# A hand-written list of steps in another order: gated linear attention on one core

## The chip, the core and the metric

The kernel runs on one core of one Trainium2 chip. The core has five engines with an instruction queue each, and each queue is worked off in its own order: TensorE (PE) for matmuls, VectorE (DVE), ScalarE (ACT) and GpSimd (POOL) for work on elements, and SyncE (SP), which here only issues DMAs. An instruction starts when its engine has come to it and the semaphores that it waits for are set. The metric is the time of one execution in microseconds (us), the median of several runs.

## The reference

```python
q_s = softmax(q, over head_dim);  k_s = softmax(k, over seq)      # with 1e-9 in the sums
kv  = einsum('bhsd,bhse->bhde', k_s, v)
x   = einsum('bhsd,bhde->bhse', q_s, kv)        # then heads side by side: (B, S, 512)
gate_pre[s] = sum over k = 0..4 of conv_w[k] * x[s + k - 4]       # causal, per channel
gate = 1 / (1 + exp(-gate_pre))
out  = (gate * (x @ w_val)) @ w_out
```

There are 8 batches, 8 heads, 576 positions and a head size of 64, all in float32.

## The kernel before

**Work and tiling.** Channels lie on partitions: the 512 channels are four blocks of 128, so x, gate, value and output of one batch are four tiles of 128 x 576 each. A batch goes through these stages: load q, k, v; maxima, exponentials and sums (`q_max`, `q_sub`, `q_exp`, `q_sum`, `k_peak`, `k_sub`, `k_exp` and others); `kv` on PE; `attend` on PE, which leaves two blocks of x in PSUM; then for each block a cast of x to the type that the large products take (`x_high`), the rest that the cast lost (`x_low`, on DVE), and the convolution. The latter is one scaled copy (`first`) and four multiply-adds (`tap`, on DVE), of which some are split into a scaled copy on ACT (`far`) and an addition on POOL (`near`). `sigmoid` follows on ACT. `value` multiplies x with `w_val` on PE, `gated` multiplies the result with the gate on DVE, `g_high` and `g_low` split this product as x was split, `project` multiplies it with `w_out` on PE, `copy` brings the result to SBUF and `put` stores it. Each of the large products takes 24 matmuls: high times low, high times high and low times high parts of four blocks, in two halves of the positions.

**The first batch differs.** Its channel blocks 0 and 1 get their convolution on PE (`conv`, 80 matmul records), and the two weight matrices are decoded from 64-bit words while it runs: eight slabs of 128 columns, 0 to 3 of `w_val` and 4 to 7 of `w_out`, each through `field`, `scaled`, `signed` (two DVE instructions), `part`, `joined`, and then `w_high` and `w_low`. Slab m is needed by `value 0 m`, or `project 0 m-4`. Twelve matmuls on ones (`warm`) stand at PE's start.

**What sets the order.** A list `ORDER` of some 1000 steps is written out in the code, and the program issues step after step as it stands there; nothing is scheduled behind it. A step is a name, a batch or slab, a block or part, and for many steps a letter for its engine: `x_high 4 1 a` casts block 1 of batch 4 on ACT, `v` stands for DVE and `p` for POOL. As every engine works off its own queue in order, the list sets for each engine what stands behind what. A second table, `HOMES`, says for each new tile which of its buffers it takes; a step that writes a buffer waits for the last reader of the tile that lay there. PSUM is four such buffers ("banks"), shared by all of PE's results, so that a product can be held up by whoever still reads the bank that it is to get: `conv`, for instance, takes the banks of x blocks 0 and 1 of batch 0 and waits for their `x_low`.

Lines that the profile names (before's numbers): `field` L282, `scaled` L204 on ACT and L206 on POOL, `signed` L291 and L292, `joined` L295, `k_raise` L380, `q_max` L415, `q_sub` L420, `q_exp` L424, `q_each` L499, `q_eps` L435, `q_mul` L506, `kv` L521, `q_turn` L546, `attend` L580, `first` L593 on ACT and L595 on DVE, `x_low` L600, `tap` L605, `value` and `project` L630, `conv_kv` L661, `conv` L676, `gated` L689, `g_low` L697. Casts and copies (`x_high`, `g_high`, `w_high`, `q_turned`, `k_turned`) are L198 on ACT and L200 elsewhere, the scalings of `copy` L204 on ACT.

Of the kernel before, what the change touches and what calls it, by code (L numbers as in the profile page):

```python
# [16 lines left out]
B, H, S, D = 8, 8, 576, 64  # L17
C = H * D
P = 128
# [22 lines left out]
    kv_sums 0, field 2 p, kv_norm 0 v, conv_kv, load_words 7, load_kc 1 2, part 2 a, q_turn 0 0, q_turned 0 0 a,
    scaled 2 p, signed 2, joined 2 p, q_turn 0 1, q_turned 0 1 a, w_high 1 a, q_max 1 0 2, attend 0 0, w_low 1 p,
    x_high 0 1 a, x_low 0 1, x_high 0 0 a, q_sub 1 1 p, x_low 0 0, q_max 1 2 4, attend 0 1, first 0 2 a, load_words 6,
    x_high 0 3 a, load_v 1, first 0 3 a, tap 0 3 3, w_high 3 p, tap 0 3 1, part 0 a, x_high 0 2 a, field 4 p,
    tap 0 3 0, q_each 1 3, conv, field 5 p, x_low 0 3, scaled 5 p, tap 0 3 2, joined 0 p, w_high 0 p, w_low 0 p,
    x_low 0 2, q_each 1 2, part 5 a, conv_gate 1, k_top 1 1, k_raise 1 1, conv_gate 0, k_top 1 3, k_raise 1 3,
    w_low 3 p, load_vt 4, k_top 1 0, k_raise 1 0, k_top 1 2, scaled 4 a, load_km 2 3, signed 5, joined 5 p,
    load_q 2 0 5, k_raise 1 2, value 0 1, q_sum 1 2 4, tap 0 2 3, w_high 2 a, value 0 0, gated 0 1, gated 0 0,
    q_sub 1 0 p, part 4 a, k_tail_turn 1, k_tail_turned 1 v, field 6 p, k_peak 2 3, q_exp 1 1 2, w_low 2 p,  # L50
    g_high 0 0 a, q_eps 1 2 4 a, q_rec 1 2 4, signed 4, k_turn 1 1, joined 4 p, k_turn 1 0, q_exp 1 0 1, q_sum 1 0 2,
    k_turned 1 0 a, load_km 3 0, q_eps 1 0 2 p, tap 0 2 0, k_peak 2 0, q_rec 1 0 2, load_k 2, g_high 0 1 a, field 7 p,
    scaled 6 a, g_low 0 0 p, k_peak 2 1, q_mul 1 0 p, w_high 5 a, value 0 2, w_high 4 a, w_low 4 p, k_turned 1 1 a,
    kv 1, q_mul 1 1 a, tap 0 2 1, tap 0 2 2, sigmoid 0 2, q_mul 1 2 p, kv_sums 1, value 0 3, g_low 0 1 p, q_mul 1 3 a,
    kv_norm 1 v, q_max 2 0 5, gated 0 2, load_km 3 2, scaled 7 a, load_km 5 3, load_v 2, q_turn 1 0, sigmoid 0 3,
    q_turn 1 1, tail_high 1 a, q_turned 1 0 a, gated 0 3, w_low 5 p, signed 6, g_high 0 2 a, g_low 0 2 v,
    g_high 0 3 a, attend 1 0, x_high 1 0 a, k_peak 3 2, first 1 0 v, g_low 0 3 p, tap 1 0 2, q_sub 2 3 p, load_kt 2,
    k_row 2, q_sub 2 4 p, tap 1 0 3, part 6 a, tap 1 0 1, q_turned 1 1 a, load_q 3 0 5, x_high 1 1 a, first 1 1 a,
    project 0 1, copy 0 1 a a, joined 6 p, q_sub 2 2 p, tap 1 0 0, project 0 0, w_high 6 a, x_low 1 0, w_low 6 p,
    load_km 5 0, tap 1 1 0, load_k 3, tap 1 1 2, put 0 1, part 7 a, x_low 1 1, signed 7, copy 0 0 a a, attend 1 1,  # L60
    project 0 2, sigmoid 1 0, far 1 2 2, x_high 1 2 a, x_high 1 3 a, joined 7 p, w_high 7 a, q_sub 2 1 p, tap 1 1 3,
    first 1 3 a, tap 1 1 1, sigmoid 1 1, w_low 7 p, k_spread 2, q_sub 2 0 p, k_sub 2 3 p, k_sub 2 1 p, k_peak 3 0,
    k_peak 5 0, k_sub 2 0 p, copy 0 2 a a, load_v 3, tap 1 3 3, x_low 1 3, x_low 1 2, value 1 0, q_exp 2 0 5, put 0 0,
    first 1 2 a, q_max 3 0 4, load_km 3 1, project 0 3, k_sub 2 4 p, gated 1 0, copy 0 3 a a, q_sum 2 0 5,
    q_eps 2 0 5 a, load_km 3 3, value 1 1, k_sub 2 2 p, put 0 2, load_km 4 3, k_peak 3 3, kt_exp 2, load_km 4 2,
    load_km 4 1, load_vt 2, k_peak 3 1, q_rec 2 0 5, k_row 3, k_exp 2, tap 1 2 0, load_km 4 0, tap 1 2 3, q_mul 2 4 a,
    q_mul 2 1 a, gated 1 1, tap 1 2 1, tap 1 3 2, tap 1 3 0, tap 1 3 1, sigmoid 1 3, g_high 1 0 p, load_km 5 1,
    q_sub 3 2 p, k_peak 4 3, value 1 3, kv 2, kv_sums 2, kv_norm 2 v, tail_turn 2, tail_turned 2 a, q_sub 3 0 p,
    k_peak 4 2, g_high 1 1 a, q_mul 2 2 p, q_mul 2 0 p, q_mul 2 3 p, q_turn 2 0, q_sub 3 1 p, g_low 1 0 p,
    q_turned 2 0 a, q_sub 3 3 p, k_peak 4 1, near 1 2 2, k_peak 5 3, put 0 3, gated 1 3, value 1 2, g_low 1 1 p,  # L70
    q_exp 3 0 4, q_turn 2 1, k_spread 3, k_peak 5 1, k_peak 4 0, sigmoid 1 2, gated 1 2, tail_high 2 a,
    q_turned 2 1 a, q_total 3, attend 2 0, far 2 1 0, first 2 0 v, tap 2 0 1, load_km 5 2, q_log 3, load_v 4,
    tap 2 0 3, load_qc 3 3, g_high 1 3 p, g_low 1 3 p, g_high 1 2 p, g_low 1 2 p, load_km 6 1, load_km 6 2, tap 2 0 2,
    l_turn 3, project 1 3, first 2 1 a, load_q 4 0 5, copy 1 3 a a, near 2 1 0, k_row 4, x_high 2 1 a, far 2 1 3,
    tap 2 1 2, put 1 3, x_low 2 1, x_high 2 0 a, x_low 2 0, load_qc 3 1, near 2 1 3, l_row 3, project 1 0,
    copy 1 0 a a, project 1 2, k_sub 3 3 p, tap 2 1 1, sigmoid 2 1, k_sub 3 4 p, far 2 0 0, k_sub 3 2 p, near 2 0 0,
    q_max 4 0 5, copy 1 2 a a, load_qc 3 0, q_sub 4 4 p, put 1 0, k_peak 6 1, attend 2 1, q_sub 4 3 p, first 2 2 a,
    tap 2 2 1, x_high 2 2 v, kt_exp 3, x_high 2 3 a, q_sub 4 1 p, first 2 3 a, tap 2 3 0, q_sub 4 2 p, x_low 2 2,
    project 1 1, copy 1 1 a a, q_sub 4 0 p, x_low 2 3, l_spread 3, sigmoid 2 0, q_exp 4 0 5, value 2 1, tap 2 2 0,
    tap 2 2 2, k_sub 3 0 p, k_sub 3 1 p, k_exp 3, load_kt 4, tail_high 3 a, l_sub 3 0 p, load_k 4, tap 2 3 1,  # L80
    gated 2 1, g_high 2 1 a, tap 2 3 3, k_peak 6 2, tap 2 3 2, k_spread 4, c_exp 3 0, value 2 0, load_qc 3 2,
    l_sub 3 3 p, g_low 2 1 p, sigmoid 2 3, gated 2 0, load_qc 4 1, value 2 3, q_total 4, c_exp 3 3, gated 2 3, kv 3,
    value 2 2, kv_sums 3, load_q 5 0 5, k_peak 5 2, tap 2 2 3, kv_norm 3 v, l_sub 3 1 p, q_log 4, c_exp 3 1,
    attend 3 0, load_km 6 3, g_high 2 0 a, sigmoid 2 2, g_high 2 3 p, g_low 2 3 p, first 3 1 a, l_turn 4, gated 2 2,
    first 3 0 v, load_vt 6, far 3 1 0, k_row 5, tap 3 0 3, g_low 2 0 p, tap 3 0 1, g_high 2 2 p, put 1 1, g_low 2 2 p,
    project 2 0, x_high 3 1 v, l_sub 3 2 p, load_km 6 0, project 2 1, load_qc 4 3, tap 3 1 2, x_low 3 1, k_sub 4 3 p,
    put 1 2, c_exp 3 2, k_sub 4 4 p, copy 2 0 a a, tap 3 1 1, tap 3 1 3, x_high 3 0 a, l_row 4, copy 2 1 a a,
    q_max 5 0 4, k_sub 4 1 p, put 2 0, far 3 0 0, attend 3 1, load_qc 5 1, first 3 3 a, k_sub 4 2 p, first 3 2 a,
    q_sub 5 1 p, k_peak 6 3, x_high 3 3 a, put 2 1, k_sub 4 0 p, project 2 2, tap 3 0 2, q_sub 5 2 p, load_qc 4 0,
    l_spread 4, x_high 3 2 a, x_low 3 0, k_exp 4, x_low 3 3, tap 3 2 3, k_peak 6 0, project 2 3, copy 2 2 a v,  # L90
# [713 lines left out]
```

## Time and profile before

| | before |
|---|---|
| median of 3 runs | 287.61 us (287.55 to 287.83) |
| the profiled execution's own time | 287.65 us |
| its span, first to last instruction | 285.9 us |
| busy PE / DVE / POOL / ACT | 278.8 / 231.7 / 205.8 / 192.8 us |
| instructions DVE / ACT / POOL | 329 / 322 / 191 |
| moved by DMA | 62.93 MB |

The span is what the trace holds; 1.75 us of the execution lie outside it. Times in the trace count from the start of the span. PE's busy time holds the time in which a matmul waits behind the one in front of it, so "busy" alone does not tell whether PE works at its pace; the distance between the starts of its groups does.

### The profile page before, as it was taken

How to read it: one execution, taken by the hardware profiler on the slowest of the kernel's cores; microseconds unless marked ns; L12 is line 12 of the kernel's file. 1: busy time of each engine (PE TensorE's matmuls, PEld its weight loads, DVE VectorE, ACT ScalarE, POOL GpSimd, SP SyncE). 2: the span in 40 equal slices, each digit the busy share in tenths (PEclk: the TensorE clock that was granted, in tenths of full speed). 3: DMA queues.
4: the chain of work that ended last, by engine and by line, in shares of the span. 5: the costliest groups of instructions: out<-in, count | busy, mean ns of one | idle time of the engine just before them, and what ended most of it. 6: DMA issues, size and time to landing. Idle time of an engine off the chain costs nothing.

```text
span 285.9 us, 6653 instructions
## 1 busy us (share of the span) xinstructions
PE 278.8 (98%) x2640; PEld 250.6 (88%) x2640; DVE 231.7 (81%) x329; ACT 192.8 (67%) x322; POOL 205.8 (72%) x191
## 2 busy tenths in 40 slices
PE   8988999999999999999999999999999999999995
...
GB/s 241 397 414 399 316 226 301 214 416 346 84 262 345 250 284 128 332 198 224 371 417 257 211 225 322 287 165 126 153 182 159 217 0 2 44 41 85 0 83 85
DMA packets 23463, 62.93 MB, mean 220 GB/s; under 512 B 3432, under 2 KB 3976, under 8 KB 20744
## 3 DMA queue, kind: packets, MB, share of 16 engines
...
q14 instruction: 10, 0.08, 0.1%
...
## 4 chain that ended last, share of the span: by engine, by line
PE 84%; DVE 7%; ACT 2%; issue 1%; POOL 1%; DVEq 0%
PE val L630 36%; PE out_a L630 32%; PE kv L521 6%; PE x L580 5%; PE cv L676 2%; DVE gate L605 2%; DVE x L600 1%; PE qTps L546 1%; DVE e L292 1%; DVE kpk L340 1%; PE kps L387 1%; ACT q L506 1%; PE out_r L630 1%; PE out_l L630 1%; POOL f L295 0%
## 5 line engine op out<-in xcount | busy, mean ns | idle before, releaser
L630 PE MATMUL val<-x,w_val_hi 128*128 128x288 f32 x512 | 89.1, 295 | 0.1
L605 DVE SCALAR_TENSOR_TENSOR gate<-x,cw,gate 128x575 f32<-128x575 f32 (+3 forms) x98 | 78.8, 809 | 5.7 <-ACT gate L593 2.2
L630 PEld LDWEIGHTS val<-x,w_val_hi 128*128 128x128 f32 x512 | 75.3, 188 | 0.3 <-DVE x L600 0.3
L630 PE MATMUL val<-x,w_val_lo 128*128 128x288 f32 x256 | 56.1, 300 | 0.0
L630 PE MATMUL out_a<-gh,w_out_lo 128*128 128x288 f32 x248 | 54.6, 301 | 0.0
L630 PE MATMUL out_a<-gh,w_out_hi 128*128 128x288 f32 x248 | 53.2, 296 | 0.0
L697 POOL TENSOR_TENSOR gl<-g,gh 128x576 fp32r<-128x576 f32 x24 | 34.6, 1443 | 14.7 <-ACT gh L198 8.0
L630 PEld LDWEIGHTS out_a<-gh,w_out_lo 128*128 128x128 f32 x248 | 39.4, 188 | 5.7 <-issue 1.8
L630 PE MATMUL out_a<-gl,w_out_hi 128*128 128x288 f32 x248 | 43.0, 295 | 0.0
L614 POOL TENSOR_TENSOR gate<-gate,far 128x572 f32<-128x572 f32 (+3 forms) x22 | 29.1, 1324 | 18.7 <-DVE gate L605 10.0
L630 PEld LDWEIGHTS val<-x,w_val_lo 128*128 128x128 f32 x256 | 40.7, 188 | 1.6 <-DVE g L689 0.4
L630 PEld LDWEIGHTS out_a<-gh,w_out_hi 128*128 128x128 f32 x248 | 39.8, 188 | 0.0
L204 ACT ACTIVATE o<-out_a 128x576 f32<-128x576 f32 x27 | 17.6, 650 | 31.6 <-PE out_a L630 22.0
L630 PEld LDWEIGHTS out_a<-gl,w_out_hi 128*128 128x128 f32 x248 | 36.4, 188 | 0.0
L420 POOL TENSOR_TENSOR q<-q,qm 128x512 f32<-128x512 f32 x32 | 33.5, 1062 | 3.6 <-DVE qm L415 3.5
L689 DVE SCALAR_TENSOR_TENSOR g<-gate,val 128x576 f32<-128x576 f32 x32 | 23.8, 749 | 13.8 <-PE val L630 5.9
L490 POOL TENSOR_TENSOR qc<-qc,lb 128x576 f32<-128x576 f32 (+1 forms) x17 | 24.1, 1428 | 11.0 <-DMA lb<-lrow 11.0
L355 POOL TENSOR_TENSOR k<-k,kmax 128x512 f32<-128x512 f32 x23 | 30.2, 1330 | 0.2
L617 ACT ACTIVATE gate<-gate 128x576 f32<-128x576 f32 x30 | 20.2, 683 | 8.3 <-DVE gate L605 8.0
L600 DVE TENSOR_TENSOR x<-x,x 128x576 fp32r<-128x576 f32 x32 | 23.1, 749 | 1.7 <-ACT x L198 1.6
L610 ACT ACTIVATE far<-x,cw 128x572 f32<-128x572 f32 (+3 forms) x22 | 16.2, 737 | 9.2 <-PE x L580 4.0
L424 ACT ACTIVATE q<-q 128x512 f32<-128x512 f32 (+2 forms) x11 | 15.9, 1442 | 8.8 <-POOL q L420 8.8
(108 smaller groups left out, 456.4 us busy)
## 6 DMA issues: line engine op xcount, KB each, us to landing
...
```

Of the source, the lines that this page charges most:

```text
L204: nc.scalar.mul(out, in_, factor)
L355: engine(e).tensor_sub(kk[r, cs], kk[r, cs], mx[r, cs])
L420: engine(e).tensor_tensor(qq, qq, m, op=ALU.add if b < 2 else ALU.subtract)
L490: engine(e).tensor_sub(t, t, T["lb", b][:, p])
L521: nc.tensor.matmul(acc[h * D:(h + 1) * D, p, :], T["k", b][:, c, cs] if c < 4 else ktz[b % 2][:, cs], T["v", b][:, c, hd] if c < 4 else T[ ...
L600: nc.vector.tensor_sub(xl, T["x", b, p], T["xh", b, p].bitcast(F32))
L605: nc.vector.scalar_tensor_tensor(out=a, in0=x, scalar=w, in1=a, op0=ALU.mult, op1=ALU.add)
L614: nc.gpsimd.tensor_add(a, a, T["far", b, p, j])
L617: nc.scalar.activation(T["gate", b, p], T["gate", b, p], AF.Tanh, scale=0.5)
L630: nc.tensor.matmul(ps[:, cs], a[:, kb, ms], z[:, cs], start=(i == 0), stop=(i == len(parts) - 1))
L689: nc.vector.scalar_tensor_tensor(out=T["g", b, m], in0=T["gate", b, m], scalar=1.0, in1=T["val", b, m], op0=ALU.add, op1=ALU.mult)
L697: engine(e).tensor_sub(T["gl", b, m], T["g", b, m], T["gh", b, m].bitcast(F32))
```

## The change

The list gets another order, and 78 of its steps another engine letter. No step is added or dropped, except that `warm` issues 11 matmuls instead of 12. Of the 78 steps, 37 come to DVE and 20 leave it, so DVE has 17 instructions more; the other 21 trade places between ACT and POOL. The list is arranged so that few `tap` steps, casts and sums stand directly behind the step whose result they read on the same engine. `HOMES` is written anew to fit the order. A second copy of the function `warm` (the same text) comes into the file; lines behind it have a number higher by five. The numbers of matmuls, DMAs and bytes stay as they are, except for that one warming matmul.

```diff
 ORDER = [step.strip() for step in """
-    warm 12, load_words 3, field 3 p, load_q 0 2 5, load_kc 0 0, load_q 0 0 1, load_taps, scaled 3 p, signed 3,
+    warm 11, load_words 3, load_q 0 2 5, load_kc 0 0, load_q 0 0 1, load_taps, load_q 0 1 2, load_ident, part 3 a,
...
-    q_mul 0 0 p, part 1 a, q_mul 0 1 a, k_peak 2 2, tail_turned 0 a, conv_rows, tail_high 0 a, joined 1 p, kv 0,
+    tail_turned 0 a, signed 0, k_peak 2 2, load_kc 1 0, kv 0, kv_sums 0, w_high 3 a, load_kc 1 1, q_mul 0 0 p,
...
 HOMES = {
     "bank": (
-        "012303102130231213213120130212310101023023102021303013021312303013012303012323021312310101231230"
-        "101203032012303013230123012"
+        "012303023012310310310302310231230303102123012120131031023132101013210323123030312020321212012103"
+        "232130301320101203023120312"
     ),
...
+    def warm(n):
+        ps = bank("warm")[:D, :512].rearrange("p (n d) -> p n d", d=D)
+        for _ in range(n):
+            nc.tensor.matmul(ps, ones, ones.unsqueeze(1).broadcast_to([P, 512 // D, D]), start=True, stop=True)
```

At three places the program's own order shows what moved. The first is DVE's start, before the change; e3 and f3 are weight slab 3 in decoding, qm the maxima of q, and q0 the first batch's q:

```order
L291 TENSOR_SCALAR e3_110<-e3_110 128x512
L292 SCALAR_TENSOR_TENSOR e3_110<-words3_108,e3_110 128x512
L415 TENSOR_REDUCE qm_0_123<-q0_112 128x8
L415 TENSOR_REDUCE qm_0_123<-q0_112 128x16
L295 ISA f3_128<-e3_110,f3_128 128x1024
```

The same place after the change:

```order
L282 TENSOR_SCALAR e3_136<-words3_107 128x512
L208 TENSOR_SCALAR e3_136<-e3_136 128x512
L291 TENSOR_SCALAR e3_136<-e3_136 128x512
L292 SCALAR_TENSOR_TENSOR e3_136<-words3_107,e3_136 128x512
L415 TENSOR_REDUCE qm_0_149<-q0_109 128x8
L415 TENSOR_REDUCE qm_0_149<-q0_109 128x16
L295 ISA f3_118<-e3_136,f3_118 128x1024
```

`field 3` and `scaled 3`, which POOL did, now stand on DVE ahead of `signed 3`.

The second place is ACT between the last `k_raise` of batch 0 and the two copies of q's transposes that `attend` reads (qT from qTps), before the change; e and f are weight slabs in decoding, qTt the tail of q:

```order
L380 ACTIVATE kc_0_3_140<-kc_0_3_140,ktop_0_131 128x576
L435 ACTIVATE qs_0_181<-qs_0_181 128x16
L198 COPY k0_237<-kps_0_0_188 128x4x256
L204 ACTIVATE e0_197<-e0_197 128x512
L204 ACTIVATE e1_249<-e1_249 128x512
L204 ACTIVATE f1_258<-words1_142 128x512
L506 ACTIVATE q0_112<-q0_112,qs_0_181 128x64 x8
L198 COPY qTt_0_270<-qTtps_0_212 128x512
L198 COPY qT_0_277<-qTt_0_270 128x4x64
L204 ACTIVATE f2_333<-words2_199 128x512
L198 COPY qT_0_277<-qTps_0_0_335 128x2x512
L198 COPY qT_0_277<-qTps_0_1_349 128x2x512
```

And after it:

```order
L380 ACTIVATE kc_0_3_126<-kc_0_3_126,ktop_0_170 128x576
L204 ACTIVATE e0_197<-e0_197 128x512
L198 COPY k0_241<-kps_0_0_210 128x4x256
L204 ACTIVATE e1_244<-e1_244 128x512
L506 ACTIVATE q0_109<-q0_109,qs_0_192 128x64 x8
L204 ACTIVATE f1_263<-words1_128 128x512
L198 COPY qTt_0_265<-qTtps_0_255 128x512
L198 CAST w_val_hi_77<-f3_118 128x4x128
L204 ACTIVATE f2_339<-words2_140 128x512
L198 COPY qT_0_345<-qTt_0_265 128x4x64
L198 COPY qT_0_345<-qTps_0_0_321 128x2x512
L198 COPY qT_0_345<-qTps_0_1_348 128x2x512
```

`q_eps` (L435) has left for DVE, and the cast `w_high 3` has come in; the rest is the same work in another order.

The third place is DVE from the sums of batch 0's kv to the two `x_low` for which `conv` waits, before the change; kvd is the normalised kv, dg the operand of `conv`, e2 weight slab 2, and x2 the two parts of x:

```order
L530 TENSOR_SCALAR ks_0_321<-kv_0_280 128x4
L531 RECIPROCAL ks_0_321<-ks_0_321 128x4
L537 TENSOR_TENSOR kvd_0_326<-kv_0_280,ks_0_321 128x256
L661 TENSOR_TENSOR dg_178<-rows_272,kvd_0_326 128x640
L291 TENSOR_SCALAR e2_324<-e2_324 128x512
L292 SCALAR_TENSOR_TENSOR e2_324<-words2_199,e2_324 128x512
L415 TENSOR_REDUCE qm_1_360<-q1_201 128x16
L600 TENSOR_TENSOR x2_0_1_373<-x_0_1_363,x2_0_1_373 128x576
L600 TENSOR_TENSOR x2_0_0_376<-x_0_0_362,x2_0_0_376 128x576
```

And after it:

```order
L530 TENSOR_SCALAR ks_0_314<-kv_0_273 128x4
L531 RECIPROCAL ks_0_314<-ks_0_314 128x4
L537 TENSOR_TENSOR kvd_0_331<-kv_0_273,ks_0_314 128x256
L282 TENSOR_SCALAR e2_333<-words2_140 128x512
L661 TENSOR_TENSOR dg_187<-rows_205,kvd_0_331 128x640
L291 TENSOR_SCALAR e2_333<-e2_333 128x512
L292 SCALAR_TENSOR_TENSOR e2_333<-words2_140,e2_333 128x512
L415 TENSOR_REDUCE qm_1_342<-q1_142 128x16
L600 TENSOR_TENSOR x2_0_1_372<-x_0_1_363,x2_0_1_372 128x576
L600 TENSOR_TENSOR x2_0_0_388<-x_0_0_362,x2_0_0_388 128x576
```

`field 2` has come from POOL to DVE, between `kv_norm` and `conv_kv`; the order is otherwise the same.

## Rows read from the trace of the kernel before

**Rows 1.** The page: busy us, share, instructions; PE's busy tenths in 40 slices

```profile
PE 278.8 (98%) x2640; PEld 250.6 (88%) x2640; DVE 231.7 (81%) x329; ACT 192.8 (67%) x322; POOL 205.8 (72%) x191
PE   8988999999999999999999999999999999999995
```

**Rows 2.** What PE waited for: total us, times, longest us

```profile
PE cv L676 <- DVE x L600: 1.1, 1, 1.1
```

**Rows 3.** The chain that ended last: start us, us, what

```profile
27.47 5.73 PE cv L676 x80
...
72.50 6.40 PE val L630 x48
78.91 2.48 PE kv L521 x80
...
86.20 0.87 PE qTps L546 x8
87.07 1.13 PE x L580 x16
...
114.59 3.40 PE val L630 x24
...
282.75 0.41 ACT o L204
```

**Rows 4.** Timeline, first 10 us: start us, us, instruction [idle before <- releaser]

```profile
4.34 0.65 POOL L282 TENSOR_SCALAR e<-words 128x512 f32<-128x512 f32 x1 [2.34 <-DMA words<-in_w_val]
...
5.73 0.43 DVE L291 TENSOR_SCALAR e<-e 128x512 int32<-128x512 int32 x1 [5.73 <-POOL e L206]
6.19 0.69 DVE L292 SCALAR_TENSOR_TENSOR e<-words,e 128x512 int32<-128x512 int32 x1
6.80 1.80 DVE L415 TENSOR_REDUCE qm<-q 128x8 f32<-128x512 f32 x2
7.56 2.54 POOL L420 TENSOR_TENSOR q<-q,qm 128x512 f32<-128x512 f32 x2 [1.87 <-DVE qm L415]
8.64 0.63 ACT L424 ACTIVATE q<-q 128x512 f32<-128x512 f32 x1 [3.68 <-POOL q L420]
```

**Rows 5.** Timeline of ACT, 14 to 26 us

```profile
14.69 2.10 ACT L380 ACTIVATE kc<-kc,ktop 128x576 f32<-128x576 f32 x3
16.96 0.21 ACT L435 ACTIVATE qs<-qs 128x16 f32<-128x16 f32 x1 [0.17 <-DVE qs L430]
17.08 0.99 ACT L198 COPY k<-kps 128x1024 f32<-128x1024 f32 x1
23.17 1.93 ACT L198 COPY qT<-qTps 128x1024 f32<-128x1024 f32 x2
24.98 0.63 ACT L198 CAST w_val_hi<-f 128x512 fp32r<-128x512 f32 x1
```

**Rows 6.** Timeline of all engines, 24 to 29 us

```profile
24.23 2.17 PE L580 MATMUL x<-qT,kvd 64*64 64x288 f32 x32 [0.23 <-ACT qT L198]
24.47 0.43 DVE L291 TENSOR_SCALAR e<-e 128x512 int32<-128x512 int32 x1 [0.55 <-POOL e L206]
25.50 1.19 ACT L198 CAST x<-x 128x576 fp32r<-128x576 f32 x2
25.54 1.21 DVE L415 TENSOR_REDUCE qm<-q 128x16 f32<-128x1024 f32 x1
26.67 1.41 DVE L600 TENSOR_TENSOR x<-x,x 128x576 fp32r<-128x576 f32 x2
28.13 1.91 PEld L676 LDWEIGHTS cv<-qT,dg 64*64 64x64 f32 x36 [0.47 <-DVE x L600]
```

**Rows 7.** Timeline of DVE and PE, 56 to 63 us

```profile
56.45 3.37 DVE L605 SCALAR_TENSOR_TENSOR gate<-x,cw,gate 128x574 f32<-128x574 f32 x4
59.73 0.75 DVE L600 TENSOR_TENSOR x<-x,x 128x576 fp32r<-128x576 f32 x1
61.20 1.20 PE L580 MATMUL x<-qT,kvd 64*64 64x288 f32 x16
```

More of the change, by code (lines that the diff above doesn't have):

```diff
@@ L42 @@
[L42 to L90, printed above, removed]
-    near 3 0 0, q_sub 5 0 p, near 3 1 0, x_low 3 2, load_k 5, load_qc 4 2, q_sub 5 3 p, tap 3 2 0, tap 3 3 2,
@@ new lines @@
+    x_high 0 1 a, x_low 0 1, attend 0 1, w_high 2 p, load_kc 1 2, x_high 0 0 a, x_low 0 0, first 0 3 a, tap 0 3 0,
+    load_words 7, load_kt 2, scaled 4 p, part 0 a, x_high 0 2 a, joined 0 p, x_high 0 3 a, q_max 1 2 4, tap 0 3 3,
+    x_low 0 3, tap 0 3 1, w_high 1 a, tap 0 3 2, q_each 1 3, x_low 0 2, w_low 1 p, w_high 0 a, q_each 1 2, field 5 p,
+    k_top 1 1, k_top 1 3, conv, scaled 5 a, w_low 2 p, load_km 2 3, conv_gate 0, conv_gate 1, first 0 2 a,
+    k_raise 1 1, w_low 0 p, part 5 p, k_top 1 0, k_raise 1 0, k_top 1 2, signed 5, joined 5 p, q_sum 1 2 4,
@@ new lines @@
+    k_raise 1 3, q_sub 1 0 p, load_v 1, part 4 a, load_vt 4, w_low 3 p, q_eps 1 2 4 a, k_raise 1 2, value 0 1,
+    gated 0 1, tap 0 2 3, value 0 0, gated 0 0, load_q 2 0 5, signed 4, joined 4 p, k_turn 1 0, q_exp 1 1 2,
+    q_exp 1 0 1, q_sum 1 0 2, k_turned 1 0 a, load_v 4, q_rec 1 2 4, g_high 0 1 a, field 7 p, k_peak 2 3,
+    g_high 0 0 a, w_high 4 a, k_tail_turn 1, tap 0 2 0, k_peak 2 0, q_mul 1 2 p, g_low 0 1 p, tail_high 1 a,
+    load_km 4 3, k_tail_turned 1 a, k_peak 2 1, q_eps 1 0 2 a, q_rec 1 0 2, w_high 5 p, k_row 2, tap 0 2 1, value 0 2,
```

174 lines of the change are left out of this document (107 added, 67 removed).

## The prediction, made before the result was known

> **What bounds the kernel now.** First the page: PE is busy 98% of the span, and its tenths are 9 in all slices but three of the first four and the last [rows 1]. Busy can hide waiting, so the waits of PE come next: the longest is 1.1 us, before `conv`, for an `x_low` on DVE [rows 2]. Then the chain that ended last, to see PE's pace [rows 3]: 48 matmuls of a product in 6.40 us, so 24, one `value` or `project`, in 3.20; a `kv` in 2.48, an `attend` in 1.13, eight transposes in 0.87; a product that stands behind a `kv` and before an `attend` takes 3.40, so a change of kind costs 0.10 on each side. From `conv` to PE's end the list holds 64 products (204.8 us), 7 `kv` (17.4), 14 `attend` (15.8), `conv` (5.7), 56 transposes (6.1) and 45 changes of kind (4.5): 254.3 us. The trace has 282.75 - 27.47 = 255.3 there. So behind `conv` at most 1.0 us of 255 is not PE's own pace.
>
> The changed list has the same matmuls behind `conv` and again 45 changes of kind. The last product is again split, and its last copy again goes to ACT (0.41 us) and is stored; what follows PE's end (285.9 - 282.75 = 3.15 us) stays, as does the 1.75 us outside the span. The time can change in two ways only: `conv` is done earlier or later, and PE is made to wait behind it, more than now or less. By the order the rest, 11 more us of DVE work or 5 fewer dependent pairs, counts only through these two.
>
> **`warm`.** One matmul fewer is two records less at PE's start. The first real matmuls wait for exponentials of k either way, so I count 0. Without that cover it would be a gain of under 1 us.
>
> **Step 1: DVE's start.** Now POOL does `field 3` (from 4.34) and `scaled 3`, DVE begins `signed 3` at 5.73 and q's maxima at 6.80 [rows 4]. In the new order DVE does all four itself from 4.34. A one-input DVE instruction on 128x512 takes 0.43 (L291), the two-input one 0.69 (L292), and one that reads what the one before wrote starts 0.03 after its end (5.73 + 0.43 to 6.19) [rows 4]: 4.34 + 3 x 0.46 + 0.69 = 6.41, and the maxima, which read none of it, may start 0.08 before that end as now (6.88 to 6.80): 6.33, that is 0.47 earlier. The trace has no `field` on DVE. Its input is every other word, as in L292; at that 0.69 the gain is 0.21, and below 0.43 nothing of this size lies. I take 0.43, the row with one input, and keep 0.21 to 0.47.
>
> [...]
>
> **Step 2: ACT to the last `k_raise`.** `q_sub` on POOL waits for those maxima (1.87) and `q_exp` on ACT for POOL (3.68) [rows 4]. From 8.64 ACT then has no gap up to the three `k_raise` at 14.69 that end at 16.79 [rows 5]; the new order has the same instructions there, one `k_raise` earlier. So 16.32, 0.47 earlier.
>
> **Step 3: ACT to q's transposes.** Now `q_eps` waits 0.17 for DVE and delays `k_turned` to 17.08; without it `k_turned` could start 0.10 before `k_raise` ends (the overlap of independent ACT instructions: 2.10 for three of 0.77 is 0.67 apart), at 16.69 [rows 5]. `q_eps` goes to DVE: 0.39 saved. `w_high 3` comes in: 0.63 less the 0.10 overlap, 0.53. `q_turned`, now at 23.17, starts 0.47 + 0.39 - 0.53 = 0.33 earlier, and so do `attend` (24.23) and the first cast of x (25.50) [rows 5, 6].
>
> **Step 4: DVE to the two `x_low`.** The cast would be done at 25.50 - 0.33 + 0.65 = 25.82. In the trace it was done about 26.15, but `x_low` came only at 26.67, since DVE was in `q_max` from 25.54, behind a `signed 2` that had waited 0.55 for POOL's `scaled 2` [rows 6]. In the new order `field 2` is on DVE ahead of `conv_kv`, so POOL can do `scaled 2` beside `conv_kv`. DVE was free at 24.47 - 0.55 = 23.92; 0.47 earlier with k, plus 0.43 - 0.08 for `field 2`, is 23.80. `signed 2` and `q_max` then take what they take now (24.47 to 26.67, 2.20 with the overlaps): 26.00. The first `x_low` starts there, the second 0.67 later, and it ends at 27.42 instead of 26.67 + 1.41 = 28.08. `conv`'s second weights wait for that end (28.13 [rows 6]); so `conv` is done 0.66 earlier. If `field` takes 0.69, steps 1 and 4 lose 0.26 each: 0.14. If the `scaled` wait stays, 0.1. If DVE is free before the cast: 28.08 - (25.87 + 0.67 + 0.75) = 0.79, the upper end. I take 0.7.
>
> **Step 5: behind `conv`.** Where the list leaves a margin I added up the instructions ahead of the releaser, from 26 us on, at the distances above. The weights come first: POOL has five instructions between `joined 2` and the `w_low 1` that `value 0 1` needs, and two more up to `w_low 0`; both end some 0.7 us ahead of PE. DVE's tap on block 0 of batch 1, the last reader of a bank that `attend 1 1` takes, ends 0.3 us ahead, where now it is 61.20 - (59.73 + 0.75) = 0.72 [rows 7]. Then DVE's margins grow to 2 to 3 us around 65 to 100 us and beyond 5 later, as ACT and POOL have slack. I count no new wait; the bounds are -1.0 (all that is loose in the body goes) and the DVE rival below.
>
> **Sum.** 287.65 (the profiled execution; the median shown is 287.61) - 0.7 + 0 = 286.9 us.
>
> **The rivals.**
> - *The front's gain is lost to the weights* (no change). The first batch's weights come through POOL, whose sums leave 0.7 us. POOL instructions of one kind vary: two `q_sub` take 2.54 us beside DVE's decoding [rows 4], where the first alone is under 1.08 (`q_exp`, behind it, begins at 8.64). One such slowing (0.4) and one wait for ACT's `part 0` and `value 0 0` starts when it does now: 287.6. For it: `joined 0` needs three engines; against it: `w_low` 1 and 0 stand early in POOL's new queue. [...]
> - *DVE becomes late* (slower). DVE gets 17 instructions more, at 0.67 us some 11 us, and each wait that I overlooked in front of `attend 1 1` beyond 0.3 us delays PE one for one; behind DVE's waiting instruction stand the taps and `x_low` of batch 1 on which `value 1 0` waits too. With 2.0 us of such waits PE loses 1.7: 286.9 + 1.7 = 288.6. From 1.6 us on it is slower by over 0.2%. For it: in that stretch `g_low 0 2` waits for a cast on ACT and `first 1 0` for `attend 1 0`, in the middle of DVE's queue. Against: DVE had margin there in a busier order, with 40 tap or `first` pairs, now 23.
> - *All waits go* (a larger gain): 286.9 - 1.0 = 285.9, if the order frees every bank in time.
>
> **How the numbers follow.** A difference under 0.2% (0.58 us) cannot be told from none here. My forecast has 0.48 (0.41 of it below 287.03, the rest within 0.2%; its own range is 286.5 to 287.4), the weights 0.25 (same), late DVE 0.19 (0.17 slower, the rest same), all waits gone 0.08. So faster 0.49, same 0.33, slower 0.18. The range leaves one in ten out on each side: 286.1 to 288.5.
>
> **What would show it.** Right: DVE's maxima of q near 6.3, ACT's three `k_raise` ending near 16.3, `q_turned` near 22.8, the second `x_low` ending near 27.4, and PE's waits without a new entry behind `conv`; the copy of the last product 0.7 us earlier, near 282.0. Wrong: `field` on DVE at 0.69 or more, `x_low` still behind a late `signed 2`, or an `attend` or `value` that waits for DVE between 33 and 65 us, which then shifts all of PE behind it.

## The result and the profile after

| | before | changed |
|---|---|---|
| median (all runs) | 287.76 us (287.55 to 288.07, 9 runs) | 290.97 us (288.91 to 295.54, 9 runs) |
| the profiled execution: time, span | 287.65, 285.9 us | 295.54, 293.8 us |

The ratio is 1.0114 with a 95% interval of 1.0078 to 1.0149: the changed kernel is slower, by 3.2 us of the median, where 0.7 us faster was forecast. Its runs also spread over 6.6 us, those of before over 0.5. The profiled execution is the longest of the nine, so its large waits are larger than in a usual run, and it doesn't divide the 3.2 us of the median; a second trace of the same kernel is in the experiments.

The page, in the form of [rows 1], with the granted clock of PE in tenths of full speed below its busy tenths:

```profile
PE 281.5 (96%) x2638; PEld 252.3 (86%) x2638; DVE 242.9 (83%) x346; ACT 188.0 (64%) x313; POOL 200.6 (68%) x183
PE   8978999999999999998999699999999999999995
PEclk9999999999999999999999889999999999999999
```

PE's tenths were 9 from the fifth slice on; now there are an 8 and a 6 near the middle, and the clock has two eights, in the slice of the 6 and in the next. What PE waited for (total us, times, longest us), in the form of [rows 2]:

```profile
PE out_a L630 <- ACT o L204: 2.3, 1, 2.3
PE out_a L630 <- DVE g L689: 1.3, 1, 1.3
...
PE cv L676 <- DVE x L600: 0.7, 1, 0.7
PE kv L521 <- DVE gate L605: 0.6, 1, 0.6
```

The wait of `conv` has shrunk from 1.1 to 0.7, and three new ones stand behind `conv`, where none was forecast.

**The front went nearly as forecast.** The rows that answer to [rows 4 to 6], from timelines (start us, us, instruction, idle before and releaser):

```profile
4.21 0.43 DVE L282 TENSOR_SCALAR e<-words 128x512 f32<-128x512 f32 x1 [4.21 <-DMA words<-in_w_val]
...
6.62 1.89 DVE L415 TENSOR_REDUCE qm<-q 128x8 f32<-128x512 f32 x2 [0.33 <-DMA q<-in_q]
14.52 2.09 ACT L380 ACTIVATE kc<-kc,ktop 128x576 f32<-128x576 f32 x3
16.73 0.68 DVE L439 TENSOR_SCALAR qs<-qs 128x16 f32<-128x16 f32 x1
...
18.16 1.20 DVE L200 COPY k<-kps 128x1024 f32<-128x1024 f32 x1
...
19.46 0.69 PE L521 MATMUL kv<-v,k 128*64 128x65 f32 x16 [0.49 <-ACT q L506]
...
21.94 1.97 PE L546 MATMUL qTps<-ident,q 128*128 128x128 f32 x16
...
22.54 0.39 ACT L198 COPY qT<-qTt 128x256 f32<-128x256 f32 x1
23.07 1.93 ACT L198 COPY qT<-qTps 128x1024 f32<-128x1024 f32 x2
...
26.16 1.41 DVE L600 TENSOR_TENSOR x<-x,x 128x576 fp32r<-128x576 f32 x2
26.96 2.35 PE L676 MATMUL cv<-qT,dg 64*64 64x288 f32 x26 [0.66 <-DVE x L600]
...
32.62 0.53 PE L630 MATMUL val<-x,w_val_lo 128*128 128x288 f32 x2
```

Two of them as they were before:

```profile
22.04 1.97 PE L546 MATMUL qTps<-ident,q 128*128 128x128 f32 x16
...
33.16 0.51 PE L630 MATMUL val<-x,w_val_lo 128*128 128x288 f32 x2
```

`field` takes 0.43 on DVE. The maxima could have started near 6.3, but waited 0.33 for q itself; the two `x_low` end at 26.16 + 1.41 = 27.57. `conv` starts at 26.96 instead of 27.47 [rows 3], and `value 0 1` at 32.62, with no wait in front of it; before it started at 33.16, so 0.54 us are won here. PE keeps that up to 100 us; at `value 1 0`, near 65 us, it gains another 0.31 by a wait that is gone.

**Then it is lost.** I compared the distance from each PE step's start to the next one's with what the same pair of kinds usually takes. From 101 us on, 13 steps have an excess. Nine have 0.16 to 0.42 each, 2.5 us together. Four are larger: `project 2 3` 1.48, `kv 4` 0.68, `project 3 2` 2.42, and `value 4 0` right behind it 1.62. With 0.62 won at the front and 0.31 at `value 1 0`: 2.5 + 6.2 - 0.9 = 7.8 us, of 295.54 - 287.65 = 7.9.

The first large one, on DVE and PE:

```profile
132.24 0.81 DVE L605 SCALAR_TENSOR_TENSOR gate<-x,cw,gate 128x575 f32<-128x575 f32 x1
136.07 0.75 DVE L340 TENSOR_REDUCE kpk<-km 128x1 f32<-128x576 f32 x1 [3.02 <-DMA km<-in_k_strided]
136.74 0.80 DVE L605 SCALAR_TENSOR_TENSOR gate<-x,cw,gate 128x572 f32<-128x572 f32 x1
137.46 0.74 DVE L689 SCALAR_TENSOR_TENSOR g<-gate,val 128x576 f32<-128x576 f32 x1
138.26 0.53 PE L630 MATMUL out_a<-gh,w_out_lo 128*128 128x288 f32 x2 [1.32 <-DVE g L689]
```

DVE stands 3.02 us at `k_peak 6 0`, a maximum that batch 6 needs only much later, for a load of k. Behind it in DVE's queue is `gated 3 0`, which frees the bank that `project 2 3` takes. The same place before:

```profile
130.14 0.81 DVE L605 SCALAR_TENSOR_TENSOR gate<-x,cw,gate 128x575 f32<-128x575 f32 x1
130.87 0.74 DVE L340 TENSOR_REDUCE kpk<-km 128x1 f32<-128x576 f32 x1
```

In the old list 38 steps stand between `load_km 6 0` and `k_peak 6 0`, and the transfer was issued 14.3 us ahead of its reader. In the new list the reader is the very next step: it was issued at 125.63, and DVE came to its reader at 136.07 - 3.02 = 133.05, only 7.4 us later. For such loads of `km` the page gives a median of 5.3 us from issue to landing; this one took 10.42. The chain of the changed kernel shows that transfer, and a store (start us, us, what):

```profile
125.63 10.42 DMA km<-in_k_strided
...
159.28 6.16 DMA out<-o
165.55 0.66 ACT o L204
166.25 4.98 PE out_a L630 x24
```

The second is the 2.42: `copy 3 1` on ACT may write its buffer of the output only when `copy 3 0`'s store from it has landed. There are two such buffers. On ACT and PE:

```profile
165.55 0.65 ACT L204 ACTIVATE o<-out_a 128x576 f32<-128x576 f32 x1 [5.61 <-DMA out<-o]
166.25 0.54 PE L630 MATMUL out_a<-gh,w_out_lo 128*128 128x288 f32 x2 [2.35 <-ACT o L204]
```

And the 1.62 behind it is the clock. Windows (stretch us, length, busy us and count of PE, PEld, DVE, ACT, POOL, then PE's granted clock, DMA share, GB/s):

```profile
160.00:166.00 6.00, 3.90 (x37) 3.05 (x36) 4.54 (x5) 0.45 (x1) 4.32 (x5) 1.00 1.03 311
166.00:172.00 6.00, 5.75 (x31) 5.75 (x32) 5.04 (x7) 3.85 (x6) 2.73 (x3) 0.72 1.06 244
172.00:180.00 8.00, 8.00 (x122) 7.77 (x121) 5.85 (x10) 6.51 (x8) 4.71 (x4) 1.00 0.74 268
```

After the idle 2.35 us PE was granted 0.72 over 6 us; from 167.50 to 170.80 it was 0.50, and there two matmuls start 0.48 us after the two in front of them (169.80 to 170.28), where 0.27 is usual (171.07 to 171.34). An estimate from the 0.72: 0.28 of 6 us, 1.7 us, is lost, about the 1.62 (1.52 against the 3.30 us that this product took before).

### The profile page after: what moved, and what is told of

Read it like the earlier page. It is cut to its first block, busy times and chain, and to the rows that moved or that the text cites. A ratio compares the mean times of both kernels' runs of the same rounds, so it can differ in the third digit from the quotient of the medians.

```text
span 293.8 us, 6635 instructions
## 1 busy us (share of the span) xinstructions
PE 281.5 (96%) x2638; PEld 252.3 (86%) x2638; DVE 242.9 (83%) x346; ACT 188.0 (64%) x313; POOL 200.6 (68%) x183
## 4 chain that ended last, share of the span: by engine, by line
PE 58%; DVE 14%; POOL 9%; DMA 8%; issue 5%; ACT 3%; SPq 1%; POOLq 0%; DVEq 0%; ACTq 0%
PE val L630 26%; PE out_a L630 20%; PE kv L521 5%; DMA km<-in_k_strided 5%; PE x L580 4%; DVE qm L415 2%; DVE gate L605 2%; DMA out<-o 2%; POOL gl L697 2%; DMA q<-in_q 2%; POOL qc L490 1%; POOL f L295 1%; POOL q L420 1%; DVE x L600 1%; ACT o L204 1%
## 5 line engine op out<-in xcount | busy, mean ns | idle before, releaser
L605 DVE SCALAR_TENSOR_TENSOR gate<-x,cw,gate 128x573 f32<-128x573 f32 (+3 forms) x98 | 77.6, 807 | 4.9 <-ACT gate L593 3.1
L630 PE MATMUL out_a<-gh,w_out_lo 128*128 128x288 f32 x248 | 55.2, 304 | 3.7 <-ACT o L204 2.3
L630 PE MATMUL out_a<-gl,w_out_hi 128*128 128x288 f32 x248 | 44.0, 300 | 0.1
L420 POOL TENSOR_TENSOR q<-q,qm 128x512 f32<-128x512 f32 x30 | 32.2, 1088 | 12.0 <-DVE qm L415 9.8
L614 POOL TENSOR_TENSOR gate<-gate,far 128x572 f32<-128x572 f32 (+3 forms) x22 | 29.7, 1357 | 11.6 <-DVE gate L605 4.5
L630 PEld LDWEIGHTS out_a<-gl,w_out_hi 128*128 128x128 f32 x248 | 37.2, 193 | 0.3 <-POOL gl L697 0.3
L355 POOL TENSOR_TENSOR k<-k,kmax 128x512 f32<-128x512 f32 x21 | 27.1, 1306 | 0.1
L600 DVE TENSOR_TENSOR x<-x,x 128x576 fp32r<-128x576 f32 x32 | 23.8, 751 | 1.2 <-ACT x L198 0.5
```

Of the source, the lines that this page charges most:

```text
L355: engine(e).tensor_sub(kk[r, cs], kk[r, cs], mx[r, cs])
L420: engine(e).tensor_tensor(qq, qq, m, op=ALU.add if b < 2 else ALU.subtract)
L600: nc.vector.tensor_sub(xl, T["x", b, p], T["xh", b, p].bitcast(F32))
L605: nc.vector.scalar_tensor_tensor(out=a, in0=x, scalar=w, in1=a, op0=ALU.mult, op1=ALU.add)
L614: nc.gpsimd.tensor_add(a, a, T["far", b, p, j])
L630: nc.tensor.matmul(ps[:, cs], a[:, kb, ms], z[:, cs], start=(i == 0), stop=(i == len(parts) - 1))
```

## The experiments

Three theories. **Margins:** the new order leaves many releasers on DVE, ACT and POOL a few tenths late, at fixed places, some 2.5 us. **Late transfers:** loads stand directly in front of their readers, and stores and loads wait in SyncE's queue for each other, so that an engine waits at a place that changes from run to run. The rival to both: **the front**, which was rearranged most (no gain from it, or a lower clock there). In the lists below only steps that moved are shown.

**The same kernel again.**

> The changed kernel once more, for a second trace and a second set of times. Theory 1 (late landings): a median of 290 to 292 us again with a wide spread, since DMA landings vary; in the new trace VectorE's k_peak 6 0 or 7 2, GpSimd's k_sub 4 4 or ScalarE's copy 3 1 again wait over 0.5 us for a DMA, and PE's waits of over 0.5 us lie between 112 and 175 us, but not all at the same steps as in the first trace. Theory 2 (thin margins alone): the waits of 0.2 to 0.4 us (value 2 1, kv 3, attend 3 1, value 5 1, project 5 2) are there again with the same sizes, and the times scatter little. Theory 3 (front): PE's granted clock is below 1.0 or new waits stand before 40 us.

Measured: 290.83 us, ratio 1.0119 (1.0091 to 1.0147). The trace is again of the longest run, 293.53. The nine small waits are there again; the large ones stand elsewhere. `project 2 3` has none; instead (timeline rows):

```profile
144.97 0.69 DVE L355 TENSOR_TENSOR k<-k,kmax 128x512 f32<-128x512 f32 x1 [1.56 <-DMA k<-in_k]
...
161.39 0.65 ACT L204 ACTIVATE o<-out_a 128x576 f32<-128x576 f32 x1 [3.47 <-DMA out<-o]
...
173.20 5.51 POOL L490 TENSOR_TENSOR qc<-qc,lb 128x576 f32<-128x576 f32 x4 [6.47 <-DMA qc<-in_q_channels]
174.65 0.68 ACT L493 ACTIVATE qT<-qc 128x576 f32<-128x576 f32 x1 [3.49 <-POOL qc L490]
...
176.74 1.47 PE L580 MATMUL x<-qT,kvd 64*64 64x288 f32 x16 [2.10 <-ACT qT L493]
```

Here `attend 5 0` waits 2.10 us, and the clock falls again (windows):

```profile
177.00:183.00 6.00, 6.00 (x43) 5.17 (x36) 5.19 (x8) 4.17 (x7) 5.92 (x6) 0.72 0.95 342
```

**Front or body.** `front_after` takes the changed list up to `value 0 0` and what is left of the old one, in its order, behind it; `body_after` the old list up to `value 2 3` (112 us) and the rest of the changed one. `HOMES` is fitted to each.

```diff
 front_after: ..., gated 0 1, tap 0 2 3, value 0 0,          (changed list up to here)
-    gated 0 0, load_q 2 0 5, signed 4, ...                  (changed list)
+    load_q 2 0 5, gated 0 0, k_tail_turn 1, ...             (what the old list still holds, in its order)
 body_after: ..., gated 2 0, load_qc 4 1, value 2 3,         (old list up to here)
+    tap 2 2 3, k_peak 5 2, q_total 4, ...                   (what the changed list still holds)
```

> The new order up to value 0 0 (39 us), the old one behind it. Theories 1 and 2, which put the whole loss behind 100 us: the front keeps its gain, conv starts near 26.96 as in the changed kernel (27.47 before), value 1 0 near 65.1, no wait of PE over 0.3 us behind conv; 287.2 us, ratio 0.998, with a spread as small as that of the kernel before (0.5 us). Theory 3 (the shorter warm, conv_rows first, or PE's clock in the front): 290 us or more with a wide spread.

> The old order up to value 2 3 (112 us), the new one behind it. Theory 1: all of the large waits are behind 112 us, so 291 to 292 us with a wide spread, and the waits of project 2 3, kv 4 and project 3 2 are there. Theory 2: a part of the thin margins lies before 112 us (value 2 1, 0.36), the rest behind: 289.5 to 290 with a small spread. Theory 3: 287.8, as the kernel before.

Measured: `front_after` 287.28, ratio 0.9992 (0.9979 to 1.0006); `body_after` 293.26, ratio 1.0192 (1.0175 to 1.0208). The loss is in the body alone, and the theory of the front falls: with the new front `conv` starts at 26.75, and no new wait stands ahead of it. Both have a wait of their own at the seam (0.73 at `value 0 3`; 1.62 at `project 2 0`), so neither measures its half cleanly.

**Single suspects.** `consumers_later` moves the three readers that stood right behind their loads.

```diff
-    load_qc 4 3, x_high 3 3 v, k_sub 4 4 p, ... load_km 6 0, k_peak 6 0, ... k_peak 7 2, k_sub 5 1 p,
+    load_qc 4 3, x_high 3 3 v, ... load_km 6 0, ... q_sub 5 0 p, k_sub 4 4 p, ... kt_exp 4, tap 3 3 2, k_peak 6 0,
+    ... tap 4 3 2, tap 4 3 3, k_peak 7 2, ...
```

> The changed kernel with three steps that read a fresh load moved back in their engine's queue: k_peak 6 0 from ahead of gated 3 0 to behind tap 3 3 2, k_sub 4 4 from ahead of q_sub 5 3 to behind q_sub 5 0, k_peak 7 2 from ahead of x_low 4 1 to behind tap 4 3 3. No load, no store and no order of loads is changed. Theory 1: the waits of project 2 3 (1.3) and kv 4 (0.6) are gone, and a part of the 2.35 of project 3 2, which stands behind a store; 288.5 to 289.5 us and a smaller spread. Theory 2: those steps are not what costs, within 0.3 us of the changed kernel. Theory 3: no difference.

Measured: 292.91, ratio 1.0181 (1.0150 to 1.0211), a miss. The waits of `project 2 3` and `kv 4` are gone, but others took their place (waits of PE):

```profile
PE out_a L630 <- ACT o L204: 2.0, 2, 1.5
PE x L580 <- DVE kvd L537: 1.3, 1, 1.3
```

So a late transfer is not cured reader by reader. `no_v` asks whether the transfers are late because there are too many bytes: the loads of v for batches 5, 6 and 7 are left out, and `kv` there reads the v of batches 4 and 3.

```diff
+        if b > 4:
+            T["v", b] = T["v", 3 if b == 7 else 4]
+            return
```

> The changed kernel without the loads of v for batches 5, 6 and 7 (each 1.04 MB; kv reads the v of batch 4 or 3 in their place, so the output differs). Every engine's order stays. Theory 1 (late landings): two of the three loads stood in SyncE's queue right ahead of the transfers that landed late (v 7 at 120.8 us, v 5 at 152.2), and 1.04 MB takes some 2.6 us at the 400 GB/s that the trace reaches; so the waits behind k_peak 6 0, k_sub 5 0, copy 3 1 and l_sub 5 1 shrink by about that, and the time falls by 1 to 2 us, to 289 to 290, with less spread. Theory 2 (thin margins between engines): 290.8, no change, as no engine's work changes.

Measured: 291.11, ratio 1.0106 (1.0091 to 1.0120), no change, another miss: three loads fewer do not change the time. `attend 4 0` waits 1.6 us there for `kv_norm 4` on DVE, which stands behind a `k_sub 5 0` that waited 1.79 us for `load_k 5`:

```profile
146.72 0.69 DVE L358 TENSOR_TENSOR k<-k,kmax 128x512 f32<-128x512 f32 x1 [1.79 <-DMA k<-in_k]
```

That load was issued at 139.54. What SyncE did shows why so late (its queue, before, changed, and `k5_early`, below; start us, us, issue):

```profile
128.69 0.60 SPq L226 DMA_DIRECT2D k<-in_k  x1
...
132.06 0.39 SPq L350 DMA_DIRECT2D kmax<-krow  x1
```

```profile
139.44 0.33 SPq L350 DMA_DIRECT2D kmax<-krow  x1
139.82 0.42 SPq L226 DMA_DIRECT2D k<-in_k  x1
```

```profile
132.33 0.44 SPq L226 DMA_DIRECT2D k<-in_k  x1
...
139.36 0.33 SPq L350 DMA_DIRECT2D kmax<-krow  x1
```

In the old list `load_k 5` stands 22 steps ahead of `k_spread 5`. In the new one it stands 13 steps behind. `k_spread 5` takes the buffer that `k_sub 4 2` still reads; this now runs on DVE behind the waiting `k_peak 6 0` (138.12 + 1.25 = 139.37), and so a load that needs nothing of it is issued at 139.8, 11 us later than before. `k5_early` moves that one load ahead.

```diff
-    g_low 3 1 p, load_k 5, q_log 5,
+    k_sub 4 2 v, load_k 5, load_qc 4 2,
```

> The changed kernel with one load moved in SyncE's queue: load_k 5 ahead of k_spread 5 and load_km 6 2 (in the traces k_spread 5 waits some 6 us for k_sub 4 2 on VectorE, and the load behind it is issued at 137.9 to 142.7 us, when VectorE and GpSimd want it at 143.4 and 144.5). Theory 1, made sharper (late because it is issued late, not because the transfers are slow): issued near 132, VectorE's wait of 1.6 to 2.4 us at k_sub 5 0 goes, PE's excess before attend 4 0 falls from 0.4 to 1.8 to 0.16; 0.2 to 1.5 us faster than the changed kernel, which has 290.8. If the transfers are slow whenever they are issued: no change there, and what moved ahead makes l_spread 4 or load_km 6 2 late instead.

Measured: 290.44, ratio 1.0082 (1.0058 to 1.0106). `k_sub 5 0` no longer waits and the excess of `attend 4 0` is gone. That the time is shorter isn't shown: the interval overlaps that of the changed kernel (1.0078 to 1.0149). The largest wait behind `conv` is now that of `project 3 2`, 1.3 us, behind a `copy 3 1` that waits 4.34 for a store. `o_three` attacks that one: a third buffer for the output, the room taken from the second buffer of `vt`, whose loads are issued later.

```diff
-    "vt": "0100",
+    "vt": "0000",
-    "o": "01101011010001011101010101101010",
+    "o": "01201201201201201201201201201201",
```

> The changed kernel with three buffers o for the copies in place of two (room for it comes from one buffer vt in place of two, for which load_vt 4 and load_vt 6 of 0.26 MB each move back). A copy then waits for the store of three products ago, 9 us and not 6 after it was issued. Theory 1 through stores: ScalarE's wait for out at copy 3 1 (3.5 to 5.6 us) and PE's before project 3 2 (0.28 to 2.42) and project 1 1 go, and the fall of PE's clock behind them (1.6); 0.5 to 2 us faster than the changed kernel, 289 to 290.3. Theory 1 through loads: that wait goes, but PE meets the next one (attend 5 0 for l_sub 5 1) and the time stays at 290.8. Theory 2: 290.8.

Measured: 289.35, ratio 1.0057 (1.0031 to 1.0082), runs from 287.67 to 294.12; the interval just overlaps that of the changed kernel. The store's wait is gone; ACT waits there for PE, as it should:

```profile
159.69 0.65 ACT L204 ACTIVATE o<-out_a 128x576 f32<-128x576 f32 x1 [2.94 <-PE out_a L630]
```

**The small waits.** `thin` moves the releaser forward, or what stands ahead of it back, at seven places, such as:

```diff
-    near 3 1 0, near 3 0 0, c_exp 3 2, attend 3 1,
+    c_exp 3 2, far 3 1 0, ... near 3 1 0, near 3 0 0, attend 3 1,
-    x_low 2 2, near 2 0 0, tap 2 3 3, ... x_low 2 3, value 2 1,
+    x_low 2 2, near 2 0 0, ... x_low 2 3, tap 2 3 3, value 2 1,
```

> The changed kernel with seven small moves at the places where each of its traces so far shows PE waiting the same 0.18 to 0.42 us: x_low 2 3 ahead of tap 2 3 3 (value 2 1, 0.35), c_exp 3 2 ahead of far 3 1 0 (attend 3 1, 0.31), k_peak 6 3 behind x_low 3 2 (value 3 0, 0.19), copy 3 0 ahead of c_exp 4 3 (project 3 1, 0.22), x_high 5 2 ahead of copy 4 1 and x_low 5 2 ahead of tap 5 2 1 (value 5 1, 0.39), g_low 5 3 on VectorE (project 5 2, 0.42), x_low 6 3 ahead of l_sub 7 3 (value 6 1, 0.18). Theory 2: these 2.0 us come back, 288.8 us. Theory 1: they come back only where no transfer is late; the late ones stay, 289 to 290 with a wide spread, and earlier copies of 3 0 and its store take some 2 us off the wait of copy 3 1.

> Both: the seven small moves, and no loads of v for batches 5, 6 and 7 (the output differs). If theories 1 and 2 together are the whole loss, it comes back together: 287 to 288 us with a spread below 1 us. If something else costs, it stays over 288.5.

Measured: `thin` 290.55, ratio 1.0093 (1.0074 to 1.0112), a miss and not clear of the changed kernel; `thin_no_v`, which has `no_v`'s edit too, 289.56, ratio 1.0054 (1.0039 to 1.0069). In `thin`'s trace the nine small waits are gone but one that my own edit made worse, `project 5 2`, behind a `g_low 5 3` that I had put on DVE (waits of PE in `thin`):

```profile
PE out_a L630 <- DVE gl L697: 1.2, 1, 1.2
...
PE out_a L630 <- ACT o L204: 0.8, 1, 0.8
```

`thin2` mends that place. The list that ran differs from the one that its expectation describes: `gated 5 2`, with `g_high 5 1` and `g_low 5 0`, stands ahead of `q_exp 7`; the steps of batch 7's logarithms were not moved.

```diff
-    gated 5 0, g_high 5 0 v, q_exp 7 0 4, q_total 7, ... k_spread 7, gated 5 2, ... first 6 1 v, g_high 5 3 v, tap 6 1 1, g_low 5 3 v,
+    gated 5 0, g_high 5 0 v, g_high 5 1 p, g_low 5 0 p, gated 5 2, q_exp 7 0 4, ... gated 5 3, g_high 5 3 v, g_low 5 3 v, first 6 1 v,
```

> The kernel with the seven small moves, with the one that misfired done otherwise: project 5 2, which there waited 2.4 us in all for g_low 5 3 in VectorE's queue, now gets gated 5 2 and kv_norm 6 ahead of l_turn 7, g_high 5 2 right behind c_exp 6 1, g_high 5 3 and g_low 5 3 right behind gated 5 3. Theories 1 and 2: 290.5 - 2.2 = 288.3 us; what is left above 287 then stands behind late transfers (copy 3 1 behind a store) and varies from run to run. If the seven places are not what costs: 290.5 as before.

> The same without the loads of v for batches 5, 6 and 7 (output differs). The trace of the kernel with the first seven moves and without these loads had one wait of PE left, 1.6 us at project 5 2, and 289.6 us median (best 288.4). Theories 1 and 2 together: with that wait gone too, 287.3 us, spread below 1 us: the gain of the front, which the prediction had at 0.7, and nothing lost behind it. If anything else costs, over 288.5.

Measured: `thin2` 290.47, ratio 1.0097 (1.0070 to 1.0124), a miss too; `thin2_no_v` 288.82, ratio 1.0035 (1.0023 to 1.0047). The wait of `project 5 2` is gone in both. `thin2` itself is no faster than `thin`: its trace has `project 3 2` behind a store again (`copy 3 1` waits 4.20) and small waits at new places (0.66 at `project 1 1`). With the loads of v left out, the moves are worth 291.11 - 288.82 = 2.3 us. That is near the 2.5 of the theory of the margins, but no clean price: of the small waits 1.4 us are left at other places, and the wait of `attend 4 0` for a transfer is gone too.

**Both together.** `fixed` computes everything and has the small moves, `load_k 5` early and three output buffers.

> The thin places moved (project 5 2 now with gated 5 2, kv_sums 6 and kv_norm 6 ahead of l_turn 7 on VectorE and g_high 5 2 behind c_exp 6 1), load_k 5 early, and three buffers o; all computed. If thin margins and late transfers are the whole loss, the front's gain is left: 287.0 to 288, and the trace has no wait of PE over 0.5 us behind 60 us. If other transfers are late in their place: 288.5 to 289.5, with new places of waits between 95 and 180 us.

Measured: 287.45 (286.69 to 291.09, 12 runs), ratio 1.0004 (0.9982 to 1.0026). The time of before is back, by sixteen moved steps (one with another engine letter) and a third buffer of the output; the front's gain, which `front_after4` below has, isn't. `fixed` keeps the changed kernel's bank table and, but for `g_low 5 3`, its engine letters, so neither that table nor DVE's 17 more instructions cost the 3.2 us by themselves. Its trace, at 288.85 a longer run, still has new places of the same two kinds (waits of PE):

```profile
PE x L580 <- DVE kvd L537: 1.0, 1, 1.0
...
PE out_a L630 <- ACT o L204: 0.7, 1, 0.7
```

**The front without its seam.** Three attempts to take out the 0.73 us that `front_after` loses where the lists meet.

```diff
 front_after2:
-    value 0 0, load_q 2 0 5, gated 0 0, k_tail_turn 1, ... signed 4, k_turn 1 1, joined 4 p, k_turn 1 0, ... value 0 2, w_high 4 a, w_low 4 p, k_turned 1 1 a,
+    value 0 0, gated 0 0, load_q 2 0 5, signed 4, joined 4 p, k_turn 1 0, k_tail_turn 1, ... k_turn 1 1, ... value 0 2, k_turned 1 1 a, w_high 4 a, w_low 4 p,
 front_after3 (against the same):
+    value 0 0, gated 0 0, load_q 2 0 5, k_turn 1 0, k_tail_turn 1, k_tail_turned 1 v, signed 4, joined 4 p, ... k_turn 1 1, ... load_k 2, k_turned 1 1 a,
 front_after4:
-    k_peak 2 0, q_rec 1 0 2, ... g_low 0 0 p, k_peak 2 1, ... tap 0 2 1, tap 0 2 2,
+    q_rec 1 0 2, ... g_low 0 0 p, ... tap 0 2 1, tap 0 2 2, k_peak 2 0, k_peak 2 1,
```

> The new order up to k_turn 1 0 (40 us) and the old one behind it, with w_high 4 behind k_turned 1 1 on ScalarE, which kv 1 waited for (0.73 us) where the two orders met in the kernel with the new front alone. The front's gain of 0.5 to 0.7 us then reaches the end, as the old body has no wait to eat it: 286.6 us, ratio 0.996, spread as before. If the old body gives no more than in the other kernel with the new front: 287.3.

> The new order up to k_turn 1 0, the old one behind it, with the two waits taken out that the seam made in the kernels with the new front (value 0 2 for k_tail_turned 1 behind signed 4 on VectorE, 1.1 us; kv 1 for k_turned 1 1 on ScalarE, 0.7). If the front's gain is real and the old body keeps it: 286.7 us, ratio 0.996, spread as before. If the seam still costs: 287.2 to 287.9.

> The new order up to value 0 0 and the old one behind it, with k_peak 2 0 and 2 1 behind tap 0 2 2 on VectorE: value 0 3 waited 0.66 us for that tap at the seam. 287.28 - 0.6 = 286.7 us, ratio 0.996, with a spread below 0.5 us, if the front's gain is kept by the old body. If taken back by another wait: 287.2.

> The same kernel as front_after4, for a second set of times. If the front's gain is real: a median of 286.9 to 287.1 again, 0.7 to 0.9 us under the kernel before on the same chip, most times within 0.5 us of each other, one or two of ten higher by 1 to 3 us. If it was chance: 287.5 or more.

Measured: `front_after2` 287.87, ratio 1.0005 (0.9996 to 1.0014); `front_after3` 287.67, ratio 0.9995 (0.9987 to 1.0004). Both only trade the seam's wait for another at `value 0 2` or `value 0 3`, 1.1 us. `front_after4` 286.97, ratio 0.9984 (0.9965 to 1.0003), and again, on another chip, 286.86 (286.76 to 287.05, 6 runs), ratio 0.9968 (0.9956 to 0.9980): 0.3% under the kernel before in the second set; the interval of the first still holds 1. Nothing over 0.5 us stands behind `conv`; ahead of it `k_turn` waits 0.8 and 1.5 us for ACT in the two traces, 0.5 before, and `conv` starts at 26.64 and 26.90 all the same. PE's other waits there, in the second trace:

```profile
PE cv L676 <- DVE x L600: 0.7, 1, 0.7
PE kv L521 <- ACT q L506: 0.5, 1, 0.5
```

## Why the prediction was wrong

**What bounds the kernel** was right: only the start of `conv` and PE's waits behind it moved the time, and the clock, which fell to 0.72 over 6 us behind two of these waits; that third way stands in no term of the sum.

**`warm`** at nothing: the first real matmuls come when they did (`k_turn 0 0` at 14.23, before at 14.32), but that was not tried by itself.

**Step 1** put `field` on DVE at 0.43: measured 0.43. Its gain of 0.47 came out as 6.80 - 6.62 = 0.18, because the load of q was the next thing to be late; I had named the cover of every instruction there, but not that of the load. The chain's own steps stand 0.46 apart (`field 3` at 4.21, `scaled 3` at 4.67), as forecast. **Step 2** carries that on: `k_raise` ended at 14.52 + 2.09 = 16.61 (forecast 16.32).

**Step 3** had another limit than it names. It follows ACT alone. ACT was free for `q_turned` at 22.54 + 0.39 = 22.93, near the forecast 22.84, but `q_turned` started at 23.07, behind PE's transposes of q. These came only 0.10 earlier than before (21.94 instead of 22.04), since `kv 0` waits at 19.46 for the bank that `k_turned 0 1` on DVE reads until 18.16 + 1.20 = 19.36 (the row names ACT, whose `q_mul` writes nothing that `kv 0` reads). And DVE was late there by `q_eps`, whose move off ACT the prediction counts as 0.39 won there: it takes 0.68 on DVE.

**Step 4** was right in kind: `x_low` stood behind `q_max` as forecast, started at 26.16 (26.00) and ended at 27.57 (27.42). The term was mis-sized, 0.5 instead of 0.7, which changes nothing in the sign. `front_after4` shows the front by itself: 1.0 us of the median when measured a second time, of which the start of `conv` (26.90 in that trace) is 0.6.

**Step 5 failed**: "I count no new wait". Two things were wrong. First, the sum took an engine's wait for a transfer as none. Loads and stores were not among the instructions that I added up, although the list moves them too: `load_km 6 0` next to its reader, `load_kt 4` from 63 to 4 steps ahead of its own, `load_k 5` behind a SyncE instruction that itself waits for DVE. DVE, ACT and POOL stop at such a place (3.02, 5.61 and 6.47 us in the rows above), and what PE needs stands behind it. `k5_early` and `o_three` each remove the wait that they aim at, and in `no_v` fewer bytes do not. Second, even without transfers nine places lack a few tenths, which durations from another order were too coarse to show; they are 2.5 us in the trace. `fixed`, which treats both, is back at the time of before. That the late transfers cost time is shown: `thin2` has small moves too and stands at 1.0097 (1.0070 to 1.0124), and `fixed`, with `load_k 5` early, the third buffer and the two later loads of `vt` that make room for it, at 1.0004 (0.9982 to 1.0026). The only other difference is a second way to order the steps around `project 5 2`, whose wait is gone in `thin2` as well. The share of the small waits is read from the trace and not shown by a run: `thin` and `thin2` alone are not clear of the changed kernel, and where the moves help, in `thin2_no_v`, a wait for a transfer goes as well. How the 3.2 us of the median divide stays open, since a wait that goes lets another one decide, as in `consumers_later`.

**The rivals.** The weights did not bind: `value 0 1` starts with no wait. DVE around `attend 1 1` was not late either: no excess there, and PE ran 0.62 us ahead through it. So the rival had the right sign and nearly the right mechanism, a waiting instruction with others behind it, but the wrong place (33 to 60 us instead of 101 us and later) and the wrong cause, dependent steps instead of transfers; its price of 1.7 us was under a half of the 290.97 - 286.9 = 4.1 us that the forecast missed. Fewer waits behind `conv` came true only at `value 1 0`, 0.31. The 5 fewer dependent pairs did not show: such an instruction starts 0.03 us behind the end of the one that it reads (4.21 + 0.43 to 4.67), where two independent `x_low` of 0.75 overlap (1.41 together), but DVE is busy 242.9 us instead of 231.7, with 17 instructions more, and is waited for where it stands at a transfer.

What stays open: which transfer is late in which run, and why single executions of nearly all these kernels come out 1 to 3 us over their median, those with the old body included (290.0 once in `front_after4`).
